# Second expert layer: output product with the activations stationary, in halves of 256 tokens

## The chip, the cores and the metric

The kernel runs on one core of a Trainium2 chip. The metric is the device time of one execution in microseconds. Before the change it took 1189.61 us, the median of three runs (1189.42 to 1192.07).

## The reference

Three stages stand one behind the other, over 8192 tokens of 192 values. The first is a windowed sum over 7 neighbouring tokens with softmax weights; then come two feed-forward layers, each 192 to 2048 to 192:

```
attn = sum over k of softmax(weight_gen)[..., k] * x[token + k - 6]     # 8 heads of 24 values
y    = leaky(attn @ w_in1) @ w_out1          # leaky(h) = max(0.01 h, h)
out  = relu(y @ w_in2) ** 2 @ w_out2
```

The weights come in double precision and the result is a float32 array of 8192 x 192.

## The kernel before

The program has a recording layer: the code does not issue instructions where it stands, but records operations with an engine, an estimated cost, a priority number and the buffers that they read and write. The planner then issues them (method `issue` of `Plan`). On TensorE the order is strictly that of the priorities; on the other engines the planner may take a later operation when the first in the list could not start yet, by its own estimates. Buffers stand in rings: tag `ph` has two PSUM buffers of two banks each, and the four accumulators `q0` to `q3` of the output product have one bank each, so all eight PSUM banks are in use.

The 8192 tokens are cut into 16 blocks `tb` of `N` = 512. A *phase* is one layer on one block; it has `NPR` = 8 *steps* `j`, and in each step 256 of the 2048 hidden values of the block are made. Phases run (layer 1, blocks 0 to 4), then layer 2 and layer 1 in turn, then layer 2 on the last five blocks: 32 phases, 256 steps. In a step,

- `mm1` multiplies the input by the hidden weights into `ph`, which has 128 partitions (hidden values) by 2 banks by 512 tokens;
- `activate` makes the activations on ScalarE: `g` exactly, `gh` rounded to the format of the products; VectorE makes the remainder `gl = g - gh`;
- `mm2`, `LAG` = 2 steps later, multiplies `gh` and `gl` by the output weights into the four accumulators.

Each factor is split into a high and a low part (suffixes h and l), and three of the four products are taken: high by high, low by high, high by low. Every product contracts over 64 partitions: matmuls come in **pairs**, one on partitions 0 to 63 and one on 64 to 127 (`HALVES`), each with its own weight load of 128 columns. `mm1` has 9 terms, thus 9 pairs in a step; `mm2` has 10 pairs, in four operations: `gh` by the high and low weights for `pa` (4 pairs), `gh` for `pb` (2), `gl` for `pa` (2), `gl` for `pb` (2). In every one of these pairs weights are stationary and 512 tokens move. A step has 19 pairs, 38 matmuls and 38 weight loads.

At the end of a layer-2 phase, `end2` copies two of the accumulators to SBUF on ScalarE, adds the other two on VectorE, moves half of one result to other partitions with a DMA, transposes both, and stores the output with six DMAs. The next phase's first `mm2` waits until the four accumulators have been read.

Of the kernel before, what the change touches and what calls it, by code (L numbers as in the profile page):

```python
# [141 lines left out]
def kernel(  # L142
# [70 lines left out]

    wi = []

    wo = []

    def weight_tiles(pool, l):
# [31 lines left out]
    def piece(kind, l, j, nj, pr, dma=False, gate=()):  # L250
        n = nj * 3 * P
        pool, rings = (sb, (("raw", 2), ("w", 4))) if l else (sg, (("raw0", 4), ("w0", 8)))
        raw = pl.buf(pool, [P, SW, 2], I32, "raw", *rings[0])
        wu = pl.buf(pool, [P, SW], F32, "wu", *rings[1])
        wa = pl.buf(pool, [P, SW], F32, "wa", *rings[1])
        first_op = len(pl.ops)
        done = Buf()
        js = slice(j, j + nj)
        for i in range(j, j + nj):
            (wi_b, wo_b)["io".index(kind)][l][i] = done  # L260

        if kind == "i":
            src = (w_in1, w_in2)[l].rearrange("(s p) (n e m) w -> p s n e (m w)", p=Q, e=2, m=P)
            for d in range(2):

                def load(d=d):
                    to = raw.t[HALVES[d], :n, :].rearrange("p (s q m) w -> p s q (m w)", s=3, m=P)
                    for q in range(nj):
                        nc.sync.dma_start(out=to[:, :, q], in_=src[:, :, j + q, d])

                pl.op("SP", 0.5 * nj, pr - 6, [], [raw], load, late=(nj * 0.6, 3.5), after=gate[:1])
        else:
            src = (w_out1, w_out2)[l].rearrange("(f p) e w -> p f e w", p=P)

            def load():
                nc.sync.dma_start(
                    out=raw.t[:, :n, :].rearrange("p (f e) w -> p f e w", e=D), in_=src[:, 2 * j : 2 * (j + nj)]
                )

            pl.op("SP", 0.5, pr - 6, [], [raw], load, late=(nj * 1.2, 3.0), after=gate[:1])  # L280

        def V(b):
            return b.t[:, :n]

        def I(b):
            return b.t[:, :n].bitcast(I32)

        pl.op(
            "ACT", act(n), pr - 3, [raw], [wu, wa],
            lambda: nc.scalar.activation(V(wu), raw.t[:, :n, 1].bitcast(F32), AF.Copy, scale=2.0**-112),  # L290
            after=gate[-1:],
        )
        pl.op(
            "DVE", dve2(n), pr - 2, [wu], [wa],
            lambda: nc.vector.tensor_scalar(  # L295
                I(wa), I(wu), 3, 0x7FFFFFF8, op0=ALU.logical_shift_left, op1=ALU.bitwise_and
            ),
        )
        pl.op(
            "DVE", dve(n), pr - 2, [wu, wa], [wa],  # L300
            lambda: nc.vector.scalar_tensor_tensor(  # L301
                I(wa), I(wu), SIGN, I(wa), op0=ALU.bitwise_and, op1=ALU.bitwise_or
            ),
        )
        pl.op(
            "DVE", dve2(n), pr - 2, [wa], [wu],
            lambda: nc.vector.tensor_scalar(I(wu), I(wa), SIGN_EXP, None, op0=ALU.bitwise_and),  # L307
        )
        pl.op(
            "DVE", dve(n), pr - 2, [wu, raw], [wu],  # L310
            lambda: nc.vector.scalar_tensor_tensor(  # L311
                V(wu), raw.t[:, :n, 0].bitcast(U32), 2.0**-52, V(wu), op0=ALU.mult, op1=ALU.mult
            ),
        )
        if dma:
            plus(wa, lambda: V(wa), wu, lambda: V(wu), pr - 2, (nj * 0.8, 4.5))
        else:
            pl.op(
                "DVE", dve(n), pr - 2, [wu, wa], [wa],
                lambda: nc.vector.tensor_tensor(V(wa), V(wa), V(wu), op=ALU.add),  # L320
            )
        def to(hl):
            if kind == "i":
                return wi[l][hl][:, :, js, :].rearrange("p s q m -> p s (q m)")
            return wo[l][:, 2 * j : 2 * (j + nj), slice(0, D) if hl == "h" else slice(D, 2 * D)]

        def val():
            return V(wa).rearrange("p (s m) -> p s m", s=3 if kind == "i" else 2 * nj)

        def high():  # L330
            if l:
                second()
            nc.scalar.copy(to("h"), val())  # L333

        hb = Buf()
        pl.op("ACT", act(n), pr - 1, [wa], [hb], high, after=tuple(borrowed) if l else ())
        parts = [(slice(None), slice(None))]
        if kind == "o":
            parts = [(slice(Q, D), slice(0, P)), (slice(0, Q), slice(P, D))]
        for ts, cs in parts:  # L340
            o = pl.op(
                "DVE", dve(n // len(parts)), pr - 1, [wa, hb], [done],
                lambda ts=ts, cs=cs: nc.vector.tensor_tensor(  # L343
                    to("l")[:, :, ts], val()[:, :, cs], to("h")[:, :, cs].bitcast(F32), op=ALU.subtract
                ),
            )
        if l == 0:
            borrowed.extend(pl.ops[first_op:])
        return o
# [4 lines left out]
    wg_flat = weight_gen.rearrange("b s h k -> (b s) (h k)").rearrange(  # L354
        "(a b i t) e -> i a b (t e)", a=A, i=BI, t=TB
    )
    out_rows = out.rearrange("(a b u) d -> a b u d", a=A, u=BI * TB)
    out_flat = out.rearrange("(a b i t) d -> i t a b d", a=A, i=BI, t=TB)
    FULL = (HALO + TB) * D

# [174 lines left out]
    g_t = {}  # L535
    acc_t = {}

    def mm1(l, tb, j, pr):
        xs = sets[l, tb]
        ph = h_t[l, tb, j] = pl.buf(ps, [P, 2, N], F32, "ph", "ph", 2)  # L540

        def go():
            wh, wl = wi[l]["h"], wi[l]["l"]

            terms = [(w, hl, s) for ss in ("ab", "s") for w, hl in ((wh, "h"), (wl, "h"), (wh, "l")) for s in ss]
            for i, (w, hl, s) in enumerate(terms):
                for d in range(2):
                    c = 2 if s == "b" else d ^ (s == "s")
                    nc.tensor.matmul(  # L549
                        ph.t[:, d, :],  # L550
                        lhsT=w[HALVES[d], c, j, :],
                        rhs=xs[s + hl].t[HALVES[d]],
                        start=(i == 0),
                        stop=(i == len(terms) - 1),
                    )

        return pl.op("PE", 9 * MM, pr, [*xs.values(), wi_b[l][j]], [ph], go)

    def activate(l, tb, j, pr):
        ph = h_t.pop((l, tb, j))  # L560
# [17 lines left out]
    def mm2(l, tb, j, pr):  # L578
# [26 lines left out]
                lambda terms=terms, g=g, n=n: prods(terms, g, first and n < 2, last and n >= 2),  # L605
            )
        if last:
            (end1, end2)[l](tb, acc, pr - 1)


    def total(acc, i, v, hold, pr):
# [7 lines left out]
    def wide(name, ring=("w", 4)):  # L619
        return pl.buf(sb, [P, N], F32, name, *ring)  # L620
# [32 lines left out]
        )  # L653
        halves(xs, "b", lambda: bu.t, bu, pr - 1)

    def end2(tb, acc, pr):
        oa, ob, bw = wide("oa", ("e", 2)), wide("ob", ("e", 2)), wide("bw")
        total(acc, 0, oa, [], pr)
        total(acc, 1, ob, [bw], pr)
        ta = pl.buf(sb, [P, N], F32, "ta", "c", 2)  # L660
        pl.op("SP", 0.5, pr, [ob], [bw], lambda: nc.sync.dma_start(out=bw.t[0:Q], in_=ob.t[Q:P]), late=(0.5, 2.0))
        pl.op("DVE", dve(N), pr + 1, [oa], [ta], lambda: nc.vector.transpose(ta.t, oa.t))

        def store(src, c0, n):
            for c in range(n):
                v = src.t[32 * c : 32 * c + 32].rearrange("a (u e) -> a u e", e=32)
                nc.sync.dma_start(out=out_rows[:, tb, :, 32 * (c0 + c) : 32 * (c0 + c + 1)], in_=v)

        pl.op("SP", 2.0, pr + 1, [ta], [], lambda: store(ta, 0, 4), late=(1.0, 2.0))
        pl.op(  # L670
            "DVE", dve(N), pr + 2, [ob, bw], [ob],
            lambda: nc.vector.tensor_tensor(ob.t[0:Q], ob.t[0:Q], bw.t[0:Q], op=ALU.add),
        )
        pl.op("DVE", dve(N), pr + 2, [ob], [oa], lambda: nc.vector.transpose(oa.t[0:Q], ob.t[0:Q]))
        pl.op("SP", 1.0, pr + 2, [oa], [], lambda: store(oa, 4, 2), late=(0.5, 2.0))


    phases = [(0, tb) for tb in range(LEAD)]
# [27 lines left out]
    with tc.manual_schedule():  # L706
# [13 lines left out]
        for i in range(len(steps) + LAG):  # L720
            if i < len(steps):
                l, tb, j = steps[i]
                q = i // NPR + 1
                if j == (LAG if i >= NPR else 0) and q < len(phases):
                    gate = starts[q - 2 : q - 1] if q > 2 else ()
                    lq, tq = phases[q]
                    if lq:
                        again(tq, at[lq, tq] - 3, gate)
                    else:
                        local_sum(tq, at[lq, tq] - (4 if tq >= EARLY else 6), gate)  # L730
                o = mm1(l, tb, j, i)
                if j == 0:
                    starts.append(o)
                activate(l, tb, j, i + 0.5)
            if i >= LAG:
                mm2(*steps[i - LAG], i + 0.5)
        pl.issue()
    Plan.last = pl

# [29 lines left out]
```

## Time and profile before

| | |
|---|---|
| median of 3 runs | 1189.61 us |
| profiled execution, its time | 1188.75 us |
| its span, first to last instruction | 1187.0 us |
| TensorE (PE) busy | 1139.3 us, 96%, 9748 matmuls |
| weight loads (PEld) busy | 919.8 us, 77%, 9748 loads |
| VectorE (DVE) busy | 725.3 us, 61% |
| ScalarE (ACT) busy | 749.3 us, 63% |
| granted TensorE clock, mean | 0.989 |

A matmul's recorded time runs from its start to the end of its pipeline, so matmuls overlap in the record: the distance between the starts of two pairs is what counts, not the duration. The same holds for weight loads. The granted clock is 1.00 (2.4 GHz) or 0.50 (1.2 GHz).

### The profile page before, as it was taken

To read this page: it belongs to the slowest core of one execution; us is meant where nothing else is said; L and a number is where in the kernel's file an instruction comes from. 1 tells how busy PE (TensorE), PEld (TensorE's weight loads), DVE (VectorE), ACT (ScalarE), POOL (GpSimd) and SP (SyncE) were. 2 spreads that over 40 slices of the span, in tenths; PEclk is the share of its full clock that TensorE was granted. 3 is DMA by queue.
4 is the path that set the end of the run, shared out by engine and by line. 5 is a ranking of instruction groups with operands and counts; after the bars stand their busy time and mean duration, and the time that the engine had idled before them with its cause. 6 is when DMAs were issued, how large, how long until landed. Compare 5 with 4: busy or idle time off the path is not lost.

```text
span 1187.0 us, 22999 instructions
## 1 busy us (share of the span) xinstructions
PE 1139.3 (96%) x9748; PEld 919.8 (77%) x9748; DVE 725.3 (61%) x871; ACT 749.3 (63%) x830; POOL 15.7 (1%) x20
## 2 busy tenths in 40 slices
PE   2699999999999999999999999999999999999997
PEld 1478787887888888788887888888788888888885
DVE  7999999848465474745648475564846543344333
ACT  2555566574756748575674857657575674777774
POOL 0210000000000000000000000000000000000000
PEclk9799999999999999999999999999999999999999
DMA  8954646051512314142131513214151231121111
GB/s 185 221 105 105 157 129 171 14 136 20 146 21 79 71 42 127 19 124 44 56 95 36 131 19 101 62 32 123 20 148 19 85 79 44 58 63 36 19 19 18
DMA packets 112798, 94.29 MB, mean 79 GB/s; under 512 B 59644, under 2 KB 89114, under 8 KB 112696
## 3 DMA queue, kind: packets, MB, share of 16 engines
q1 hardware_dynamic: 108712, 87.99, 29.6%
q0 software_dynamic: 3792, 4.72, 2.5%
q8 instruction: 76, 1.25, 0.4%
q14 instruction: 26, 0.21, 0.1%
q10 hardware_dynamic: 192, 0.11, 0.0%
HBM read 50.06 MB, written 20.19 MB: 59 GB/s over the span
## 4 chain that ended last, share of the span: by engine, by line
PE 90%; DVE 6%; issue 1%; ACT 1%; DMA 1%; SPq 0%; POOL 0%; DVEq 0%; POOLq 0%; ACTq 0%
PE ph L549 43%; PE pa L591 29%; PE pb L591 19%; DVE gl L574 1%; DVE tmp L471 1%; DVE att L483 1%; DVE wa L301 1%; DVE wu L311 0%; DVE wu L307 0%; DVE wa L295 0%; DMA xc<-in_x_dram 0%; DVE wo L343 0%; DMA wg<-in_weight_gen_dram 0%; ACT wu L290 0%; DMA bw<-ob 0%
## 5 line engine op out<-in xcount | busy, mean ns | idle before, releaser
L574 DVE TENSOR_TENSOR gl<-g,gh 128x1024 fp32r<-128x1024 f32 x256 | 312.7, 1223 | 391.0 <-ACT g L571 292.7
L566 ACT ACTIVATE gh<-ph 128x1024 fp32r<-128x1024 f32 x128 | 131.7, 1029 | 262.3 <-PE ph L549 262.3
L591 PE MATMUL pa<-gh,wo 64*128 64x512 f32 x2048 | 280.3, 392 | 2.0 <-DVE s L615 1.9
L591 PEld LDWEIGHTS pa<-gh,wo 64*128 64x128 f32 x2048 | 191.5, 185 | 50.0 <-DVE oa L615 3.5
L569 ACT ACTIVATE g<-ph 128x1024 f32<-128x1024 f32 x128 | 131.6, 1028 | 119.7 <-PE ph L549 119.7
L591 PE MATMUL pa<-gl,wo 64*128 64x512 f32 x1024 | 159.9, 390 | 0.6 <-DVE gl L574 0.6
L591 PE MATMUL pb<-gh,wo 64*128 64x512 f32 x1024 | 159.9, 390 | 0.0
L591 PE MATMUL pb<-gl,wo 64*128 64x512 f32 x1024 | 159.5, 389 | 0.0
L571 ACT ACTIVATE g<-g 128x1024 f32<-128x1024 f32 x128 | 136.1, 1063 | 3.5
L570 ACT ACTIVATE gh<-g 128x1024 fp32r<-128x1024 f32 x128 | 135.7, 1060 | 4.0
L567 ACT ACTIVATE g<-ph 128x1024 f32<-128x1024 f32 x128 | 130.7, 1021 | 0.2 <-DVE gl L574 0.2
L591 PEld LDWEIGHTS pa<-gl,wo 64*128 64x128 f32 x1024 | 96.1, 184 | 22.9 <-DVE gl L574 1.1
L591 PEld LDWEIGHTS pb<-gh,wo 64*128 64x128 f32 x1024 | 96.1, 184 | 22.3 <-DVE wo L343 0.5
L591 PEld LDWEIGHTS pb<-gl,wo 64*128 64x128 f32 x1024 | 96.2, 184 | 21.9
L471 DVE TENSOR_TENSOR tmp<-xc,wg 128x768 f32<-128x768 f32 x96 | 91.1, 949 | 0.0
L483 DVE TENSOR_TENSOR att<-att,tmp 128x768 f32<-128x768 f32 x91 | 86.9, 955 | 1.7
L549 PE MATMUL ph<-xah,wi0h 64*128 64x512 f32 x256 | 52.4, 405 | 8.9 <-ACT wi0h L333 8.9
L549 PE MATMUL ph<-xah,wi0l 64*128 64x512 f32 x256 | 52.4, 405 | 2.5 <-DVE wi0l L343 2.5
L549 PE MATMUL ph<-xbl,wi0h 64*128 64x512 f32 x256 | 51.8, 401 | 0.9 <-DVE xbl L406 0.9
L549 PE MATMUL ph<-xbh,wi0l 64*128 64x512 f32 x256 | 51.9, 402 | 0.0
L549 PE MATMUL ph<-xbh,wi0h 64*128 64x512 f32 x256 | 51.6, 400 | 0.0
L549 PE MATMUL ph<-xal,wi0h 64*128 64x512 f32 x256 | 51.6, 399 | 0.0
(98 smaller groups left out, 1450.7 us busy)
## 6 DMA issues: line engine op xcount, KB each, us to landing
xc<-in_x_dram SPq DMA_DIRECT2D x62, 240.0 KB, 4.5
xsh<-xah SPq DMA_DIRECT2D x60, 128.0 KB, 2.4
xsl<-xal SPq DMA_DIRECT2D x60, 128.0 KB, 2.4
raw<-in_moe_w_in_dram SPq DMA_DIRECT2D x32, 192.0 KB, 6.3
raw<-in_moe_w_out_dram SPq DMA_DIRECT2D x7, 768.0 KB, 4.8
sc<-xb SPq DMA_DIRECT2D x14, 384.0 KB, 2.3
ka<-s SPq DMA_DIRECT2D x16, 256.0 KB, 2.0
kb<-s SPq DMA_DIRECT2D x16, 256.0 KB, 3.1
```

What stands on the lines that cost most here:

```text
L301: lambda: nc.vector.scalar_tensor_tensor(I(wa), I(wu), SIGN, I(wa), op0=ALU.bitwise_and, op1=ALU.bitwise_or),
L471: nc.vector.tensor_tensor(dst, xk, wg.t[:, :, :, k : k + 1].to_broadcast([P, TB, H, G]), op=ALU.mult)
L483: lambda tmp=tmp: nc.vector.tensor_tensor(acc(), acc(), tmp.t, op=ALU.add),
L549: nc.tensor.matmul(ph.t[:, d, :], lhsT=w[HALVES[d], c, j, :], rhs=xs[s + hl].t[HALVES[d]], start=(i == 0), stop=(i == len(terms) - 1),)
L566: pl.op("ACT", W, pr, [ph], [gh], lambda: nc.scalar.activation(gh.t, ph.t, AF.Prelu, alpha=0.01))
L567: pl.op("ACT", W, pr, [ph], [g], lambda: nc.scalar.activation(g.t, ph.t, AF.Prelu, alpha=0.01))
L569: pl.op("ACT", W, pr, [ph], [g], lambda: nc.scalar.activation(g.t, ph.t, AF.Relu))
L570: pl.op("ACT", W, pr, [g], [gh], lambda: nc.scalar.activation(gh.t, g.t, AF.Square))
L571: pl.op("ACT", W, pr, [g], [g], lambda: nc.scalar.activation(g.t, g.t, AF.Square))
L574: lambda: nc.vector.tensor_tensor(gl.t, g.t, gh.t.bitcast(F32), op=ALU.subtract),
L591: nc.tensor.matmul(acc[d][w == "b"].t, lhsT=wt[:, {"ah": slice(0, P), "b": slice(P, 2 * P), "al": slice(2 * P, 3 * P)}[w]], rhs=g.t[HALVES ...
```

## The change

In layer 2 alone, the output product turns its factors round: 128 tokens of the activations become the stationary operand, and the output weights move, 384 columns for `gh` (192 high and 192 low) and 192 for `gl` (the high ones). The results come out with tokens on partitions, so the transposes at the end fall away. An accumulator now holds 128 tokens by 384 columns; the four of them hold 256 tokens, in the two partition halves' parts `d`. So layer 2 works on halves `u` of 256 tokens: in a step, `mm1` makes the hidden values of two former steps (512 of them) for 256 tokens, by 18 pairs of 256 columns each, and four steps complete a half. `mm2_turned` has 8 pairs of 384 columns and 8 of 192. The new `end2` runs twice in a phase.

```diff
@@ piece: no reordering of the low weights in layer 2
-        if kind == "o":
+        if kind == "o" and l == 0:
@@ mm1
+    def parts(l, j):
+        if l == 0:
+            return [(slice(0, N), j, slice(0, N))]
+        u, jj = divmod(j, NPR // 2)
+        return [(slice(HN * e, HN * e + HN), 2 * jj + e, slice(HN * u, HN * u + HN)) for e in range(2)]
...
-            for i, (w, hl, s) in enumerate(terms):
...
-                    nc.tensor.matmul(
-                        ph.t[:, d, :],
-                        lhsT=w[HALVES[d], c, j, :],
-                        rhs=xs[s + hl].t[HALVES[d]],
...
+            for to, jw, cols in parts(l, j):
+                for i, (w, hl, s) in enumerate(terms):
...
+                        nc.tensor.matmul(
+                            ph.t[:, d, to],
+                            lhsT=w[HALVES[d], c, jw, :],
+                            rhs=xs[s + hl].t[HALVES[d], cols],
...
@@ new: the output product of layer 2
+    def mm2_turned(tb, j, pr):
+        gh, gl = g_t.pop((1, tb, j))
+        u, jj = divmod(j, NPR // 2)
+        first, last = jj == 0, jj == NPR // 2 - 1
...
+        jobs = [(e, c) for e in range(2) for c in range(2)]
+        def prods(q, g, width, begin, end):
+            for i, (e, c) in enumerate(jobs):
+                for d in range(2):
+                    o = HN * e + P * q
+                    nc.tensor.matmul(
+                        acc[d][q].t[:, 0:width],
+                        lhsT=g.t[HALVES[d], c, o : o + P],
+                        rhs=wo[1][HALVES[d], 2 * (2 * jj + e) + c, 0:width],
...
+        for n, (g, width, cost) in enumerate(((gh, 2 * D, 0.176), (gl, D, 0.107))):
+            for q in range(2):
+                pl.op(
+                    "PE", 4 * cost, pr + 0.02 * n + 0.01 * q, [g, *ws], [a[q] for a in acc],
+                    lambda q=q, n=n, g=g, width=width: prods(q, g, width, first and n == 0, last and n == 1),
+                )
+        if last:
+            end2(tb, u, acc, pr - 1)
@@ end2, new: twice per phase, for 256 tokens
+    def end2(tb, u, acc, pr):
+        v = pl.buf(sb, [P, 2, 2 * D], F32, "v", "w", 4)
+        for q in range(2):
+            pl.op(
+                "ACT", act(2 * D), pr, [acc[1][q]], [v],
+                lambda q=q: nc.scalar.copy(v.t[:, q], acc[1][q].t[:, 0 : 2 * D]),
+            )
+        for q in range(2):
+            pl.op(
+                "DVE", dve(2 * D), pr, [acc[0][q], v], [v],
+                lambda q=q: nc.vector.tensor_tensor(v.t[:, q], acc[0][q].t[:, 0 : 2 * D], v.t[:, q], op=ALU.add),
+            )
+        pl.op(
+            "DVE", dve(2 * D), pr, [v], [v],
+            lambda: nc.vector.tensor_tensor(v.t[:, :, 0:D], v.t[:, :, 0:D], v.t[:, :, D:], op=ALU.add),
+        )
...
+                nc.sync.dma_start(out=out_flat[2 * u + q][:, :, tb], in_=v.t[:, q, 0:D])
```

On TensorE, in the middle of a layer-2 phase, one step stands so before: nine input pairs (`ph`, here by their two matmuls, x2), then the output product (`pa`, `pb`) of two steps earlier. Sizes are partitions by moving columns.

```order
L549 MATMUL ph<-xal,wi1h 128x512 x2
L549 MATMUL ph<-xbl,wi1h 128x512 x2
L549 MATMUL ph<-xsh,wi1h 128x512 x2
L549 MATMUL ph<-xsh,wi1l 128x512 x2
L549 MATMUL ph<-xsl,wi1h 128x512 x2
L591 MATMUL pa<-gh,wo_1025 128x512 x8
L591 MATMUL pb<-gh,wo_1025 128x512 x4
L591 MATMUL pa<-gl,wo_1025 128x512 x4
L591 MATMUL pb<-gl,wo_1025 128x512 x4
```

And so after the change, from the fifth pair of the step's second set of nine (the first set, the same nine rows, stands ahead of it):

```order
L561 MATMUL ph<-xal,wi1h 128x256 x2
L561 MATMUL ph<-xbl,wi1h 128x256 x2
L561 MATMUL ph<-xsh,wi1h 128x256 x2
L561 MATMUL ph<-xsh,wi1l 128x256 x2
L561 MATMUL ph<-xsl,wi1h 128x256 x2
L637 MATMUL po<-wo_1025,gh 128x384 x16
L637 MATMUL po<-wo_1025,gl 128x192 x16
```

The step goes from 38 matmuls with as many weight loads to 68; the order of the two products against each other stays.

On ScalarE, in the middle of a layer-2 phase of the changed kernel, the two accumulator copies of the first half (`v<-po`) stand between the second and the third activation of a step:

```order
L581 ACTIVATE g<-ph 128x1024
L582 ACTIVATE gh<-g 128x1024
L583 ACTIVATE g<-g 128x1024
L581 ACTIVATE g<-ph 128x1024
L582 ACTIVATE gh<-g 128x1024
L706 COPY v<-po 128x384 x2
L583 ACTIVATE g<-g 128x1024
```

Before, no copy stood in the middle of a phase there; the one set of copies stood behind the phase's last step, among the next phase's activations, where the second half's copies stand now too.

On VectorE the last instructions of the program were these before (`ob<-ob,bw` adds what the DMA brought, and two transposes stand around it):

```order
L574 TENSOR_TENSOR gl<-g,gh 128x1024 x6
L615 TENSOR_TENSOR oa<-pa,oa 128x512
L615 TENSOR_TENSOR ob<-pb,ob 128x512
L662 STREAM_TRANSPOSE ta<-oa 128x512
L672 TENSOR_TENSOR ob<-ob,bw 64x512
L674 STREAM_TRANSPOSE oa<-ob 64x512
```

and are these after:

```order
L586 TENSOR_TENSOR gl<-g,gh 128x1024 x4
L711 TENSOR_TENSOR v<-po,v 128x384 x2
L715 TENSOR_TENSOR v<-v 128x2x192
L586 TENSOR_TENSOR gl<-g,gh 128x1024 x3
L711 TENSOR_TENSOR v<-po,v 128x384 x2
L715 TENSOR_TENSOR v<-v 128x2x192
```

The transposes and the wait for a DMA are gone from the end, and the short sums stand there twice, once for each half of 256 tokens.

## Rows read from the trace of the kernel before

**Rows 1.** The page: span, and busy time by engine (share of the span, instructions).

```profile
span 1187.0 us, 22999 instructions
...
PE 1139.3 (96%) x9748; PEld 919.8 (77%) x9748; DVE 725.3 (61%) x871; ACT 749.3 (63%) x830; POOL 15.7 (1%) x20
```

**Rows 2.** The page: chain that ended last, by engine and by line.

```profile
PE 90%; DVE 6%; issue 1%; ACT 1%; DMA 1%; SPq 0%; POOL 0%; DVEq 0%; POOLq 0%; ACTq 0%
PE ph L549 43%; PE pa L591 29%; PE pb L591 19%; DVE gl L574 1%; DVE tmp L471 1%; DVE att L483 1%; DVE wa L301 1%; DVE wu L311 0%; DVE wu L307 0%; DVE wa L295 0%; DMA xc<-in_x_dram 0%; DVE wo L343 0%; DMA wg<-in_weight_gen_dram 0%; ACT wu L290 0%; DMA bw<-ob 0%
```

**Rows 3.** Timeline of PE, two layer-2 steps (start us, us, engine, line, form).

```profile
596.57 0.39 PE L549 MATMUL ph<-xah,wi1h 64*128 64x512 f32 x2
...
600.87 0.39 PE L549 MATMUL ph<-xah,wi1h 64*128 64x512 f32 x2
...
605.18 0.39 PE L549 MATMUL ph<-xah,wi1h 64*128 64x512 f32 x2
```

**Rows 4.** Timeline of PE, layer 1, eight pairs apart.

```profile
566.04 0.39 PE L549 MATMUL ph<-xbh,wi0h 64*128 64x512 f32 x2
...
567.91 0.40 PE L591 MATMUL pa<-gh,wo 64*128 64x512 f32 x2
```

**Rows 5.** Timeline of PE at the start of the program, four pairs apart.

```profile
36.99 0.62 PE L549 MATMUL ph<-xbh,wi0l 64*128 64x512 f32 x2
...
38.69 0.63 PE L549 MATMUL ph<-xsh,wi0l 64*128 64x512 f32 x2
```

**Rows 6.** Windows (stretch, length, busy of PE, PEld, DVE, ACT, POOL, clock, DMA share, GB/s).

```profile
36.50:39.00 2.50, 2.50 (x12) 2.01 (x14) 2.46 (x6) 0.00 (x0) 1.21 (x1) 0.50 1.09 251
...
550.00:576.00 26.00, 26.00 (x224) 20.72 (x222) 22.16 (x28) 12.95 (x15) 0.00 (x0) 1.00 0.12 21
1040.00:1170.00 130.00, 130.00 (x1150) 107.45 (x1148) 52.63 (x56) 100.73 (x104) 0.00 (x0) 1.00 0.16 32
```

**Rows 7.** Timeline of PE and PEld after a wait at full clock: one pair, two pairs.

```profile
52.24 0.19 PEld L591 LDWEIGHTS pa<-gl,wo 64*128 64x128 f32 x2 [1.08 <-DVE gl L574]
52.24 0.30 PEld L591 LDWEIGHTS pa<-gl,wo 64*128 64x128 f32 x4 [1.08 <-DVE gl L574]
52.24 0.50 PE L591 MATMUL pa<-gl,wo 64*128 64x512 f32 x2 [0.64 <-DVE gl L574]
```

**Rows 8.** Timeline, the program's first weight load and first matmul.

```profile
21.53 0.18 PEld L496 LDWEIGHTS pt<-ident,att 128*128 128x128 f32 x1 [21.53 <-issue]
...
21.56 0.45 PE L496 MATMUL pt<-ident,att 128*128 128x128 f32 x1 [21.56 <-DVE att L483]
```

**Rows 9.** Groups by line and shape, adds and copies at a layer-2 phase's end (busy, mean ns).

```profile
L615 DVE TENSOR_TENSOR oa<-pa,oa 128x512 f32<-128x512 f32 x16 | 11.0, 686 | 11.1 <-ACT oa L612 11.1
...
L612 ACT COPY oa<-pa 128x512 f32<-128x512 f32 x16 | 9.3, 583 | 3.1 <-PE pa L591 3.1
```

**Rows 10.** Waits in total (us, times, longest), weight loads for the accumulators.

```profile
PEld pa L591 <- DVE oa L615: 3.5, 11, 0.3
```

**Rows 11.** Timeline of a step's end in layer 2: input product, activation.

```profile
1166.63 0.39 PE L549 MATMUL ph<-xsl,wi1h 64*128 64x512 f32 x2
...
1167.06 1.03 ACT L569 ACTIVATE g<-ph 128x1024 f32<-128x1024 f32 x1 [1.09 <-PE ph L549]
```

**Rows 12.** Timeline: weights for the next windowed sum, their load and first use.

```profile
601.28 1.98 SPq L423 DMA_DIRECT2D wg<-in_weight_gen_dram  x4
...
619.62 0.38 DVE L447 TENSOR_REDUCE mx<-wg 128x32 f32<-128x224 f32 x1
```

**Rows 13.** Timeline of the last microseconds, all engines.

```profile
1177.51 0.61 PE L591 MATMUL pb<-gl,wo 64*128 64x512 f32 x4
...
1179.54 0.70 DVE L662 STREAM_TRANSPOSE ta<-oa 128x512 f32<-128x512 f32 x1
...
1181.99 0.68 DVE L672 TENSOR_TENSOR ob<-ob,bw 64x512 f32<-64x512 f32 x1 [1.75 <-DMA bw<-ob]
...
1183.44 0.85 SPq L667 DMA_DIRECT2D out_dram<-oa  x2
```

More of the change, by code (lines that the diff above doesn't have):

```diff
@@ L356 @@
     )
-    out_rows = out.rearrange("(a b u) d -> a b u d", a=A, u=BI * TB)
     out_flat = out.rearrange("(a b i t) d -> i t a b d", a=A, i=BI, t=TB)
@@ L536 @@
     acc_t = {}
+    HN = N // 2
+    def parts(l, j):
[3 more added lines that the diff above has]
+        return [(slice(HN * e, HN * e + HN), 2 * jj + e, slice(HN * u, HN * u + HN)) for e in range(2)]
     def mm1(l, tb, j, pr):
@@ L545, in go @@
             terms = [(w, hl, s) for ss in ("ab", "s") for w, hl in ((wh, "h"), (wl, "h"), (wh, "l")) for s in ss]
-            for i, (w, hl, s) in enumerate(terms):
-                for d in range(2):
-                    c = 2 if s == "b" else d ^ (s == "s")
-                    nc.tensor.matmul(
-                        ph.t[:, d, :],
-                        lhsT=w[HALVES[d], c, j, :],
-                        rhs=xs[s + hl].t[HALVES[d]],
[L553 to L557, printed above, removed]
+            for to, jw, cols in parts(l, j):
+                for i, (w, hl, s) in enumerate(terms):
+                    for d in range(2):
+                        c = 2 if s == "b" else d ^ (s == "s")
+                        nc.tensor.matmul(
+                            ph.t[:, d, to],
+                            lhsT=w[HALVES[d], c, jw, :],
+                            rhs=xs[s + hl].t[HALVES[d], cols],
+                            start=(i == 0),
+                            stop=(i == len(terms) - 1),
+                        )
+        return pl.op("PE", 9 * MM, pr, [*xs.values(), *(wi_b[l][jw] for _, jw, _ in parts(l, j))], [ph], go)
     def activate(l, tb, j, pr):
@@ L607, in mm2 @@
         if last:
-            (end1, end2)[l](tb, acc, pr - 1)
+            end1(tb, acc, pr - 1)
+    def mm2_turned(tb, j, pr):
+        gh, gl = g_t.pop((1, tb, j))
+        u, jj = divmod(j, NPR // 2)
+        first, last = jj == 0, jj == NPR // 2 - 1
+        if first:
+            acc_t[1] = [[pl.buf(ps, [P, N], F32, "po", f"q{2 * d + q}", 1) for q in range(2)] for d in range(2)]
+        acc = acc_t[1]
+        jobs = [(e, c) for e in range(2) for c in range(2)]
+        def prods(q, g, width, begin, end):
+            for i, (e, c) in enumerate(jobs):
+                for d in range(2):
+                    o = HN * e + P * q
[3 more added lines that the diff above has]
+                        rhs=wo[1][HALVES[d], 2 * (2 * jj + e) + c, 0:width],
+                        start=begin and i == 0,
+                        stop=end and i == len(jobs) - 1,
+                    )
+        ws = [wo_b[1][2 * jj + e] for e in range(2)]
+        for n, (g, width, cost) in enumerate(((gh, 2 * D, 0.176), (gl, D, 0.107))):
[6 more added lines that the diff above has]
+            end2(tb, u, acc, pr - 1)
     def total(acc, i, v, hold, pr):
@@ L654, in again, with store @@
         halves(xs, "b", lambda: bu.t, bu, pr - 1)
[L656 to L669, printed above, removed]
+    def end2(tb, u, acc, pr):
[9 more added lines that the diff above has]
+                lambda q=q: nc.vector.tensor_tensor(v.t[:, q], acc[0][q].t[:, 0 : 2 * D], v.t[:, q], op=ALU.add),
+            )
         pl.op(
-            "DVE", dve(N), pr + 2, [ob, bw], [ob],
-            lambda: nc.vector.tensor_tensor(ob.t[0:Q], ob.t[0:Q], bw.t[0:Q], op=ALU.add),
-        )
-        pl.op("DVE", dve(N), pr + 2, [ob], [oa], lambda: nc.vector.transpose(oa.t[0:Q], ob.t[0:Q]))
-        pl.op("SP", 1.0, pr + 2, [oa], [], lambda: store(oa, 4, 2), late=(0.5, 2.0))
+            "DVE", dve(2 * D), pr, [v], [v],
+            lambda: nc.vector.tensor_tensor(v.t[:, :, 0:D], v.t[:, :, 0:D], v.t[:, :, D:], op=ALU.add),
+        )
+        def store():
+            for q in range(2):
+                nc.sync.dma_start(out=out_flat[2 * u + q][:, :, tb], in_=v.t[:, q, 0:D])
+        pl.op("SP", 1.0, pr + 1, [v], [], store, late=(0.5, 2.0))
     phases = [(0, tb) for tb in range(LEAD)]
@@ L735 @@
             if i >= LAG:
-                mm2(*steps[i - LAG], i + 0.5)
+                l, tb, j = steps[i - LAG]
+                if l:
+                    mm2_turned(tb, j, i + 0.5)
+                else:
+                    mm2(l, tb, j, i + 0.5)
         pl.issue()
```

## The prediction, made before the changed kernel ran

> **What bounds the kernel now.** I read the page first: TensorE is busy 96% of the span, and 90% of the chain that ended last lies on it, all of that on the two product lines [rows 1, 2]. VectorE and ScalarE stand near 60% over the span. In the stretch that is layer 2 alone, ScalarE works 100.73 of 130 us (77%) and VectorE 52.63 (40%), with TensorE busy throughout and the clock at 1.00 [rows 6]. So a layer-2 step is worth what its pairs of matmuls cost, as long as the others keep up.
>
> The timeline gives that cost. Two layer-2 steps take 605.18 - 596.57 = 8.61 us [rows 3]; a step is 4.305 us, and with 19 pairs a pair takes **226.6 ns**. In layer 1 eight pairs take 1.87 us, 234 ns each, with the same shapes at the same full clock [rows 4, 6]. At the half clock (1.2 GHz) four pairs take 1.70 us, 425 ns each [rows 5, 6]; 512 columns at 1.2 GHz are 426.7 ns, so there the stream of columns is all that counts. At 2.4 GHz the stream would be 213.3 ns. So at full clock each pair carries a **surcharge** over its stream: 13.3 ns in layer 2 and about 20.5 ns in layer 1.
>
> Is it a price per column or per weight load? Layers 1 and 2 differ in these pairs in where the weights lie and in the numbers themselves; counts, widths and the moving tiles' rings are alike. A difference of 7 ns that follows the weights points to the load. I therefore take the surcharge as one per pair, whatever its width. This is the main choice in the sum.
>
> A second floor shows where the array resumes after a wait at full clock. The first pair is recorded 0.50 us long instead of the usual 0.39, so its columns began 0.11 us after its load; and two pairs' loads end 0.30 us after the first's start while one takes 0.19, so the second load began 0.11 us after the first [rows 7]. A pair thus can't come sooner than about **110 ns** after the one ahead of it, the time in which its weights get ready.
>
> **The sum, part by part.**
>
> *Input product.* 9 pairs of 512 columns become 18 of 256, with twice the loads. 256 columns stream in 106.7 ns; with 13.3 a pair takes 120 ns, just over the load's floor. 18 x 120 = 2.160 us, against 9 x 226.6 = 2.039: **+0.121 us** a step.
>
> *Output product.* 10 pairs of 512 become 8 of 384 (160 + 13.3 = 173.3 ns) and 8 of 192 (80 + 13.3 = 93.3, so the floor of 110 holds). 1.387 + 0.880 = 2.267 us against 2.266: **nothing**. The columns fall from 5120 to 4608, and the six more loads eat it.
>
> So a step goes from 4.305 to 4.426 us; over 128 layer-2 steps that is **+15.5 us**.
>
> *Stationary activations.* The output product's loads now read `gh` and `gl`, which no load of before does. The two values known are 13.3 and 20.5 ns; the floor covers them for the narrow pairs (80 + 20.5 is under 110). On 8 wide pairs the upper value is 7.2 x 8 x 128 = 7.4 us; I take the middle, **+3.7 us**.
>
> Here the Trainium skill speaks for the change: its page "TensorE: Matmul & The Clock Gate", section Back-to-back issue gap, prices an isolated matmul at full clock at its columns over 2.4 GHz plus 2.5 ns, that is 109, 162.5 and (by the load) 110 ns for the three widths. By it a step would be 4.14 us, and the sum some 24 us under before. The trace does not agree at 512 columns: the page's 215.8 ns are 226.6 in rows 3.
>
> *ScalarE and VectorE.* A half's four accumulators need two copies and two adds of 384 columns, and one add of 2 x 192. ScalarE's order puts the copies behind the second activation of a step. With T for the start of the input product's last pair, the first activation starts at T + 0.43 and takes 1.03 [rows 11]; two such end near T + 2.5; the output product that closes the half ends about then. Two copies (under 0.58 each, the price at 512 columns) and two adds (under 0.69) [rows 9] overlap each other, so the first bank is free near T + 3.8 and the second near T + 4.4. The next half's first output product starts one input product later, near T + 0.1 + 2.27 + 2.16 = T + 4.5, and reaches its second bank 0.7 us after that. No wait, therefore, but slack of some 0.7 us; if the copies slipped behind the third activation (1.03 us), about 0.4 us would be lost at 16 places, 6 us. At the phase's end the accumulators' old wait, 3.5 us in 11 waits [rows 10], stays at most. ScalarE gains some 0.7 us per phase, which its 23% of free time covers. These cost nothing in the sum.
>
> *Transfers.* Six stores and a copy by DMA per phase become four stores; the DMA engines are 16% busy there [rows 6]. SyncE issues in order, and the first half's stores now stand ahead of the loads for the next windowed sum. They wait for a half that ends some 29 us into the phase, against 22 us, where the first of those loads (`wg`) was issued before; `wg` was first read 18 us after that [rows 12]. The slack covers the 7 us.
>
> *The end.* Now 9.0 us lie between the last pair's start (1177.51 + about 0.45) and the end of the span at 1187.0: an add, a transpose, a DMA round trip that VectorE waits 1.75 us for, an add, a transpose, a store [rows 13]. After: copy (0.55), add (0.6), short sum (0.55), two stores issued, and the same 2.7 us from the last issue's end (1184.3) to the end of the span. With 0.8 for the issues and the first matmul tail this is about 6 us: **-3 us**.
>
> Sum against the profiled execution's own 1188.75 us: +15.5 + 3.7 - 3 = +16.2, **1205 us**. The profiled execution lies 0.9 us under the median of the runs, which I let stand.
>
> **The rivals.**
>
> *The surcharge goes with the columns, or fades (faster).* If 13.3 ns on 512 columns is 2.6 ns per hundred, pairs take 113.3, 170 and 110 ns: a step of 4.28 us, -3.2 - 3 = 1182.5 us. If it vanished for all three widths, with the floor of 110 left: 1.98 + 1.28 + 0.88 = 4.14 us, 1165 us. It decides for faster where the surcharge on the 26 wider pairs is under 9.5 ns: 18 x (106.7 + s) + 8 x (160 + s) + 880 = 4305 + 23 (the end's 3 us per step). For it: no row shows a narrow pair at full clock. Against it: layer 1 against layer 2.
>
> *The dear loads (slower still).* With layer 1's 20.5 ns on all wider pairs a step is 18 x 127.2 + 8 x 180.5 + 880 = 4.61 us: +39.5 - 3, 1225 us. Instructions could bind at the same height: the program's first matmul follows its load by 0.03 us [rows 8]; four instructions to a pair are 0.12 us, 68 x 2 x 0.03 = 4.1 us a step, hidden just now; at 0.034 us each they would be the bound.
>
> *A load must end before the next pair (far slower).* Recorded loads last 0.19 us [rows 7]. Were that, with 3 ns to the next start, the least distance, 34 pairs at 0.19 make 6.5 us a step: +2.15 x 128, about 1460 us. Against it stands the second load of rows 7, which began before the first had ended.
>
> The same page and section of the Trainium skill names a rule on this side: in a sustained stream of loads and matmuls it gives 81 ns per matmul at 128 columns and 131 at 512, so that narrow ones hardly get cheaper. By it, scaled to the 113 ns per matmul of this trace, a step would rise by about 1.55 us, to 1387 us. No run here shows such a floor yet.
>
> *No change.* A surcharge near 9.5 ns, or the end gaining more: 1186 to 1193 us.
>
> **How the numbers follow.** Chances: the forecast (surcharge 13 to 18 ns per pair, 1195 to 1214 us) 0.48; dear loads or instructions (1214 to 1245) 0.14; load must end 0.03; no change 0.08; per column or fading (1160 to 1186) 0.27. A measurement of this kernel tells 0.3%, 3.6 us, from no change. So faster 0.27, same 0.08, slower 0.65. The likeliest case has its own range of 1195 to 1214; the range for 8 in 10 takes in most of the faster case and of the dearer one, 1170 to 1240.
>
> **What would show it.** In the changed trace's timeline: the distance of pairs in a layer-2 step, 0.120 us for 256 columns, 0.173 for 384, 0.110 for 192; a step of 4.43 us; no new wait of TensorE on the copies (L706) or adds (L711); layer 1's 234 ns as before; about 6 us from the last matmul to the end. The forecast is wrong if 256-column pairs stand at 0.113 us or less, or if the loads or the sequencer hold the narrow pairs above 0.13 us.

## The result, and the profile after

The changed kernel takes **1202.64 us** (median of 4 runs, 1202.22 to 1205.76), the kernel before 1190.84 on the same chip (1189.42 to 1193.33). The ratio is 1.011, with a 95% interval of 1.0094 to 1.0127: slower by 1.1%, and inside the range of the forecast. The execution that was profiled is the longest of the four, 1205.76 us; where its last 3 us come from is read below.

The page of the changed kernel: its span, the busy time of the engines, and the chain that ended last, by engine and by line (of before: [rows 1, 2]).

```profile
span 1204.0 us, 30628 instructions
...
PE 1157.0 (96%) x13588; PEld 1079.5 (90%) x13588; DVE 725.6 (60%) x883; ACT 757.1 (63%) x862; POOL 15.7 (1%) x20
...
PE 91%; DVE 6%; issue 1%; ACT 1%; DMA 0%; SPq 0%; POOL 0%; DVEq 0%; POOLq 0%; ACTq 0%
PE ph L561 44%; PE po L637 24%; PE pa L603 14%; PE pb L603 9%; DVE gl L586 1%; DVE tmp L471 1%; DVE att L483 1%; DVE wa L302 1%; DVE wu L312 0%; DVE wu L308 0%; DVE wa L296 0%; DMA xc<-in_x_dram 0%; DVE wo L344 0%; ACT wu L291 0%; DVE wi0l L344 0%
```

TensorE bounds it as before, and by as much of its span. It runs 3840 matmuls more, and its weight loads take 90% of the span instead of 77%. So the question is again what a pair costs. TensorE's timeline over one step of layer 2 shows it (start, us, line, form; it answers to [rows 3]):

```profile
1180.77 1.57 PE L637 MATMUL po<-wo,gh 64*128 64x384 f32 x16
1182.16 1.05 PE L637 MATMUL po<-wo,gl 64*128 64x192 f32 x16
1183.03 0.33 PE L561 MATMUL ph<-xah,wi1h 64*128 64x256 f32 x2
1183.17 0.30 PE L561 MATMUL ph<-xbh,wi1h 64*128 64x256 f32 x2
...
1185.09 0.30 PE L561 MATMUL ph<-xsl,wi1h 64*128 64x256 f32 x2
1185.20 0.36 PE L637 MATMUL po<-wo,gh 64*128 64x384 f32 x2
```

Eight wide pairs take 1182.16 - 1180.77 = 1.39 us, 174 ns each. Eight narrow ones take 0.87 us, 109 ns each. The 18 input pairs take 2.17 us: 120 ns each, but the first, behind the narrow ones, 0.14 us. The step is 4.43 us, where it was 4.305. The output product alone is as long as before (2.26 against 2.27 us); the input product is longer by 0.13. Layer 1's steps take 4.45 us, as before.

Two windows of the changed kernel, the stretch of [rows 6] in layer 2, and one early in the program (stretch, length, busy of PE, PEld, DVE, ACT, POOL, clock, DMA share, GB/s):

```profile
80.00:90.00 10.00, 8.00 (x50) 6.07 (x52) 8.91 (x12) 4.08 (x7) 0.00 (x0) 0.83 0.00 0
...
1040.00:1170.00 130.00, 130.00 (x1998) 130.00 (x1996) 51.11 (x59) 99.70 (x109) 0.00 (x0) 1.00 0.12 34
```

and the early window of the kernel before:

```profile
80.00:90.00 10.00, 9.16 (x74) 7.28 (x76) 9.90 (x13) 4.89 (x7) 0.00 (x0) 1.00 0.01 2
```

In layer 2 TensorE waits for nothing at full clock, and VectorE, ScalarE and the DMA engines do a little less than before. The early window, where the program is the same, differs by itself: TensorE is busy for 1.16 us less, and its mean clock is 0.83. One input product of layer 1 and the output product behind it show what that costs, in the changed kernel and in the kernel before:

```profile
83.31 0.73 PE L561 MATMUL ph<-xah,wi0h 64*128 64x512 f32 x2
87.06 1.09 PE L603 MATMUL pa<-gh,wo 64*128 64x512 f32 x8
```

```profile
81.51 0.50 PE L549 MATMUL ph<-xah,wi0h 64*128 64x512 f32 x2
83.72 1.10 PE L591 MATMUL pa<-gh,wo 64*128 64x512 f32 x8
```

The product begins 1.80 us later, behind longer waits, and takes 3.75 us instead of 2.21. These 3.3 us are the whole difference at the first step of layer 2, which begins at 230.90 us, in the profile before at 227.61. They are no part of what layer 2 does; in the traces of runs 1, 2 and 3 below, whose layer 1 is unchanged too, that step begins at 233.34, 229.45 and 227.99 us.

ScalarE and VectorE at the point where a half closes in mid-phase, in the changed kernel (in brackets the idle time ahead, and what ended it):

```profile
1182.05 1.06 ACT L582 ACTIVATE gh<-g 128x1024 fp32r<-128x1024 f32 x1
1183.01 0.84 ACT L706 COPY v<-po 128x384 f32<-128x384 f32 x2
1183.74 1.07 ACT L583 ACTIVATE g<-g 128x1024 f32<-128x1024 f32 x1
1183.51 1.02 DVE L711 TENSOR_TENSOR v<-po,v 128x384 f32<-128x384 f32 x2 [2.49 <-ACT v L706]
1184.56 0.56 DVE L715 TENSOR_TENSOR v<-v 128x384 f32<-128x384 f32 x1
```

The copies stand behind the second activation, as ordered, and both accumulators are read by 1183.51 + 1.02 = 1184.53. The next half's first output pair starts at 1185.20. So TensorE has at least 0.67 us to spare; the first pair's operation needs only the first two accumulators, and the add that reads the last of them ends at 1184.06, 1.14 us ahead. No wait of TensorE on L706 or L711 is on the list of waits.

The last microseconds of the changed kernel (of before: [rows 13]):

```profile
1196.27 0.40 PE L637 MATMUL po<-wo,gl 64*128 64x192 f32 x4
1196.27 0.93 ACT L706 COPY v<-po 128x384 f32<-128x384 f32 x2 [3.19 <-PE po L637]
1196.78 1.02 DVE L711 TENSOR_TENSOR v<-po,v 128x384 f32<-128x384 f32 x2 [2.44 <-ACT v L706]
1197.84 0.56 DVE L715 TENSOR_TENSOR v<-v 128x384 f32<-128x384 f32 x1
1198.42 1.12 SPq L720 DMA_DIRECT2D out_dram<-v  x2
```

From the last matmul's end (1196.67) to the end of the span are 7.3 us; by the same reading it was 8.9. The copies and adds are as short as reckoned. The two issues took 1.12 us instead of 0.8, and 4.4 us pass from the end of the last issue (1199.54) to the end of the span, where 2.7 did.

The account of the profiled executions: from the first layer-2 step's start to the last matmul's end 965.8 us against 950.5, +15.3; the end -1.6; the start +3.3. Together that is the 17.0 us between the spans.

### The profile page after: what moved, and what is told of

It is laid out like the page before. It is cut to its first block, busy times and chain, and to the rows that moved or that the text cites. A ratio compares the mean times of both kernels' runs of the same rounds, so it can differ in the third digit from the quotient of the medians.

```text
span 1204.0 us, 30628 instructions
## 1 busy us (share of the span) xinstructions
PE 1157.0 (96%) x13588; PEld 1079.5 (90%) x13588; DVE 725.6 (60%) x883; ACT 757.1 (63%) x862; POOL 15.7 (1%) x20
## 4 chain that ended last, share of the span: by engine, by line
PE 91%; DVE 6%; issue 1%; ACT 1%; DMA 0%; SPq 0%; POOL 0%; DVEq 0%; POOLq 0%; ACTq 0%
PE ph L561 44%; PE po L637 24%; PE pa L603 14%; PE pb L603 9%; DVE gl L586 1%; DVE tmp L471 1%; DVE att L483 1%; DVE wa L302 1%; DVE wu L312 0%; DVE wu L308 0%; DVE wa L296 0%; DMA xc<-in_x_dram 0%; DVE wo L344 0%; ACT wu L291 0%; DVE wi0l L344 0%
## 5 line engine op out<-in xcount | busy, mean ns | idle before, releaser
L637 PE MATMUL po<-wo,gh 64*128 64x384 f32 x2048 | 202.4, 333 | 0.0
L637 PEld LDWEIGHTS po<-wo,gh 64*128 64x128 f32 x2048 | 178.6, 185 | 0.9
L603 PE MATMUL pa<-gh,wo 64*128 64x512 f32 x1024 | 145.3, 397 | 1.9 <-DVE s L660 1.8
L637 PE MATMUL po<-wo,gl 64*128 64x192 f32 x2048 | 134.7, 268 | 0.0
L637 PEld LDWEIGHTS po<-wo,gl 64*128 64x128 f32 x2048 | 134.7, 187 | 0.0
L603 PEld LDWEIGHTS pa<-gh,wo 64*128 64x128 f32 x1024 | 103.3, 186 | 18.6 <-DVE s L660 2.7
L561 PE MATMUL ph<-xah,wi1h 64*128 64x256 f32 x512 | 80.3, 288 | 0.0
L561 PE MATMUL ph<-xbl,wi1h 64*128 64x256 f32 x512 | 78.2, 280 | 0.0
L561 PE MATMUL ph<-xsl,wi1h 64*128 64x256 f32 x512 | 78.2, 280 | 0.0
L561 PE MATMUL ph<-xbh,wi1l 64*128 64x256 f32 x512 | 78.2, 280 | 0.0
```

The lines of the kernel that those rows point to most:

```text
L561: nc.tensor.matmul(ph.t[:, d, to], lhsT=w[HALVES[d], c, jw, :], rhs=xs[s + hl].t[HALVES[d], cols], start=(i == 0), stop=(i == len(terms) - 1),
L603: nc.tensor.matmul(acc[d][w == "b"].t, lhsT=wt[:, {"ah": slice(0, P), "b": slice(P, 2 * P), "al": slice(2 * P, 3 * P)}[w]], rhs=g.t[HALVES ...
L637: nc.tensor.matmul(acc[d][q].t[:, 0:width], lhsT=g.t[HALVES[d], c, o : o + P], rhs=wo[1][HALVES[d], 2 * (2 * jj + e) + c, 0:width], start= ...
```

## The experiments

Theory: the loss is the halving of the input product, at about 13 ns for each pair, however wide. Rivals: the new output product costs time and something else gives it back; the surcharge goes with something other than pairs; the layers' 234 and 226.6 ns have a cause that changes what the loss rests on.

**1. The input product in halves, and nothing else** (from the kernel before).

```diff
+            spans = [slice(0, N // 2), slice(N // 2, N)] if l else [slice(0, N)]
+            for cols in spans:
...
-                        ph.t[:, d, :],
+                            ph.t[:, d, cols],
...
-                        rhs=xs[s + hl].t[HALVES[d]],
+                            rhs=xs[s + hl].t[HALVES[d], cols],
```

> The kernel before with one part of the change: layer 2's input product alone goes in 18 pairs of 256 columns instead of 9 of 512 (each pair of before cut in two, with its weights loaded twice); the output product, its end and the order of the work stay as before. Theory (a surcharge of 13.3 ns per pair, whatever its width): pairs at 120 ns instead of 226.6, +0.12 us in each of 128 layer-2 steps, +15 us, about 1206 us. Rival (the surcharge goes with the columns): 113 ns, 0 us. Rival (the output product is what made the changed kernel slower): 0 us here.

Measured: 1210.24 us, ratio 1.0165 (1.015 to 1.0181). TensorE's timeline of this kernel, one layer-2 step:

```profile
600.98 1.09 PE L593 MATMUL pa<-gh,wo 64*128 64x512 f32 x8
...
603.27 0.28 PE L551 MATMUL ph<-xah,wi1h 64*128 64x256 f32 x2
603.38 0.28 PE L551 MATMUL ph<-xbh,wi1h 64*128 64x256 f32 x2
...
605.42 0.40 PE L593 MATMUL pa<-gh,wo 64*128 64x512 f32 x2
```

18 pairs take 605.42 - 603.27 = 2.15 us, 0.11 over the nine of before, and the output product ahead of them 603.27 - 600.98 = 2.29 us, 0.02 more than before. A phase of eight steps is 1.00 us longer (35.64 against 34.65): 16 us over the 16 phases, a little more than the changed kernel's 15.3. The other 4 us or so (5.7 in the profiled executions) lie ahead of layer 2, whose first step begins at 233.34 us. There TensorE stood idle for longer and then ran at the half clock (window of this kernel):

```profile
80.00:90.00 10.00, 6.80 (x30) 4.82 (x32) 9.75 (x14) 4.08 (x7) 0.00 (x0) 0.66 0.00 0
```

SyncE's issues of the first weights for the windowed sum took 3.76 us there, against 1.81 before and 2.65 in the changed kernel; what lengthened them stays open, since that part of the program is not changed.

**2. Narrow pairs cut in half** (from the changed kernel; half of the products with `gl` is left out).

```diff
-        for n, (g, width, cost) in enumerate(((gh, 2 * D, 0.176), (gl, D, 0.107))):
+        for n, (g, width, cost) in enumerate(((gh, 2 * D, 0.176), (gl, D // 2, 0.107))):
```

> The changed kernel with half of the work of the narrow pairs left out: the low activations multiply 96 of the 192 weight columns (half of that correction is missing from the output). Theory (a pair can't come sooner than 110 ns after the last, the time in which its weights get ready): pairs stay at about 109 ns, no change, 1203 us. Rival (192 columns' stream plus a surcharge of 28 ns): 40 ns less on 8 pairs in 128 steps, 41 us faster, about 1162 us.

Measured: 1203.51 us, ratio to before 1.0108 (1.0094 to 1.0123), the time of the changed kernel. Its timeline:

```profile
1178.86 1.58 PE L637 MATMUL po<-wo,gh 64*128 64x384 f32 x16
1180.25 1.01 PE L637 MATMUL po<-wo,gl 64*128 64x96 f32 x16
...
1181.26 0.31 PE L561 MATMUL ph<-xbh,wi1h 64*128 64x256 f32 x2
...
1183.30 0.51 PE L637 MATMUL po<-wo,gh 64*128 64x384 f32 x3
```

The step is 1183.30 - 1178.86 = 4.44 us with half of the narrow columns gone, and from the second on narrow pairs still stand 108 to 112 ns apart. The second starts 46 ns behind the first, and the first input pair behind them takes as much longer: from the first narrow pair to the second input pair it is 1.01 us here (1181.26 - 1180.25) and in the changed kernel (1183.17 - 1182.16). The floor that [rows 7] showed holds: below some 110 ns a pair gets no cheaper.

**3. The turned output product over whole blocks and all 128 rows** (from the kernel before): the input product stays at 512 columns, and single matmuls take the place of pairs.

```diff
+                nc.tensor.matmul(
+                    acc[q].t[:, 0:width],
+                    lhsT=g.t[:, c, P * q : P * q + P],
+                    rhs=wo[1][:, 2 * j + c, 0:width],
...
+                if l:
+                    mm2_turned(tb, j, i + 0.5)
```

> The other part of the change alone: layer 2's output product is turned round, but contracts over 128 partitions in one matmul instead of two pairs of 64, so that four accumulator banks hold a whole block of 512 tokens and the input product keeps its 9 pairs of 512 columns. Per step 8 matmuls of 384 and 8 of 192 columns with 16 loads, where the changed kernel has twice as many over 64 partitions. Theory (one load and its stream count once, however many partitions): output product 2.27 us as before and in the changed kernel, the end some 2 us shorter: 1186 to 1190 us. Rival (changing between products over 64 and over 128 partitions empties the array, twice a step): 0.2 us or more each, 50 us slower or worse. Rival (one matmul instead of two saves the surcharge): 8 x 11 ns x 128 = 11 us faster, 1177 us.

Measured: 1240.76 us, ratio 1.0421 (1.0407 to 1.0436). Its timeline, an output product and the input product behind it:

```profile
611.56 1.68 PE L665 MATMUL po<-wo,gh 128*128 128x384 f32 x8
613.07 1.03 PE L665 MATMUL po<-wo,gl 128*128 128x192 f32 x8
614.03 0.50 PE L549 MATMUL ph<-xah,wi1h 64*128 64x512 f32 x2
614.37 0.39 PE L549 MATMUL ph<-xbh,wi1h 64*128 64x512 f32 x2
614.60 0.40 PE L549 MATMUL ph<-xah,wi1l 64*128 64x512 f32 x2
...
615.98 0.39 PE L549 MATMUL ph<-xsl,wi1h 64*128 64x512 f32 x2
616.30 0.44 PE L665 MATMUL po<-wo,gh 128*128 128x384 f32 x1
```

Single matmuls over 128 rows stand as far apart as the pairs (177 and 112 ns), so the output product is no dearer by its width. But each change between 64 and 128 rows is paid on both of its sides. The first input pair takes 0.34 us and the last 0.32, where one takes 0.227; the eight wide matmuls take 1.51 us, where 8 x 177 ns are 1.42, and the eight narrow ones 0.96, where 8 x 112 are 0.90. The input product grows from 2.04 to 2.27 us and the output product by as much: some 0.4 us a step, so about 0.2 us for each of its two changes, and about 50 us in all. The Trainium skill says that a change of tiling mode drains the array ("TensorEngine Tiling (Array Packing)", section Tiling Modes) and gives no price; the delay of 0.2 us at each change agrees with it.

**4. Layer 1's weights shifted by 32 bytes** (from the kernel before). The forecast rests on a reading of the two layers' 234 and 226.6 ns; the next runs ask what that difference is.

```diff
+    const.tile([P, 8], F32, name="gap0")
     weight_tiles(const, 0)
+    const.tile([P, 8], F32, name="gap1")
```

> The kernel before with nothing changed but the place of layer 1's three weight tiles in SBUF, 32 bytes further on (two unused tiles of 32 bytes around them, so that all else moves by 64). Layer 1's weights lay at multiples of 64 bytes, layer 2's, the inputs and the activations lie 32 bytes off such multiples. Theory (the surcharge comes from the weight load, and the 7 ns between the layers from where the weights lie): layer 1's pairs fall from 234 to 227 ns, 19 x 128 x 7.3 ns = 18 us off, about 1172 us. Rival (the numbers in the tiles, or what else runs beside layer 1): no change, 1190 us.

Measured: 1188.04 us, ratio 0.998 (0.9969 to 0.9991). A layer-1 step still takes 565.74 - 561.31 = 4.43 us, where it was 4.45. The shift took off some 2 us, not the 18 of this theory, which fell:

```profile
561.31 0.39 PE L551 MATMUL ph<-xah,wi0h 64*128 64x512 f32 x2
...
565.74 0.40 PE L551 MATMUL ph<-xah,wi0h 64*128 64x512 f32 x2
```

**5. Layer 1's input product in halves** (from the kernel before; the edit of run 1, for layer 1 alone).

```diff
+            spans = [slice(0, N // 2), slice(N // 2, N)] if l == 0 else [slice(0, N)]
```

> The kernel before with layer 1's input product, not layer 2's, cut into 18 pairs of 256 columns. Layer 1's pairs of 512 columns carry 20.5 ns over their stream. Theory (all of a surcharge is per pair): pairs at 127 ns, +0.18 us in 128 steps, 23 us slower, about 1213 us. Rival (13.3 per pair as in layer 2, the further 7 ns with the columns): 123.6 ns, +0.12 us, 16 us slower, 1206 us. Rival (the further 7 ns come only at 512 columns): 120 ns, +0.05 us, 7 us slower, 1197 us.

Measured: 1193.55 us, ratio 1.0026 (1.0011 to 1.004). Its timeline, an input product of layer 1:

```profile
561.47 0.28 PE L551 MATMUL ph<-xah,wi0h 64*128 64x256 f32 x2
561.59 0.28 PE L551 MATMUL ph<-xbh,wi0h 64*128 64x256 f32 x2
...
563.58 1.10 PE L593 MATMUL pa<-gh,wo 64*128 64x512 f32 x8
```

18 pairs take 2.11 us here, and 2.13 in the mean of layer 1's steps, where nine took 2.11 before. Halving costs layer 1 next to nothing, because its pairs of 256 columns lose the extra 7 ns that its pairs of 512 carry: they stand 115 to 121 ns apart, not 127. With 118 ns in the mean they carry 11 ns over their stream of 106.7, even less than layer 2's.

**6. Layer 1's weights placed behind the other tiles** (from the kernel before). Inputs and activations move down by the weights' 48 KB in each partition.

```diff
-    weight_tiles(const, 0)
     wi_b = [[None] * NPR for _ in range(2)]
...
+    weight_tiles(ctx.enter_context(tc.tile_pool(name="const0", bufs=1)), 0)
     stage = ExitStack()
```

> The kernel before with layer 1's three weight tiles in another part of SBUF: from byte 130848 of each partition on, above the inputs and activations and below layer 2's weights, instead of from 17536 on, below them; the inputs and activations move down by 49152 bytes, nothing else changes. The move by 32 bytes left layer 1's pairs at 233 ns. Theory (the 7 ns between the layers come from the part of SBUF in which the weights lie): layer 1's pairs fall to about 227 ns, up to 18 us off, 1172 us. Rival (not the place, but the numbers or the layer's other work): layer 1 stays at 233 to 234 ns, 1190 us.

Measured: **1174.36 us**, ratio 0.9865 (0.9842 to 0.9889). Its timeline, a layer-1 step:

```profile
540.89 0.39 PE L549 MATMUL ph<-xah,wi0h 64*128 64x512 f32 x2
...
542.93 1.07 PE L591 MATMUL pa<-gh,wo 64*128 64x512 f32 x8
...
545.20 0.39 PE L549 MATMUL ph<-xah,wi0h 64*128 64x512 f32 x2
```

The step takes 4.31 us, layer 2's own price: nine pairs in 2.04, ten in 2.27. Layer 1's extra cost was one of placement, and this kernel beats both.

**7. Only layer 1's output weights placed there** (from the kernel before). It asks whether the cost goes with the stationary tile itself.

```diff
-    weight_tiles(const, 0)
+    wi.append({k: const.tile([P, 3, NPR, P], F32R, name=f"wi0{k}") for k in "hl"})
...
+    wo.append(ctx.enter_context(tc.tile_pool(name="const0", bufs=1)).tile([P, NFC, 2 * D], F32R, name="wo0"))
```

> The kernel before with only layer 1's output weights moved up (from byte 155424 on); its input weights stay at 17536, below the inputs and activations, which move down by 24576 bytes. Theory (each pair's surcharge follows the place of its own stationary tile): layer 1's output pairs fall to 227 ns, its input pairs stay near 233; about 10 x 128 x 7 ns = 9 us off, 1181 us. Rival (it is the place of the moving tiles, which also moved): both products change alike, all of 16 us or nothing.

Measured: 1184.46 us, ratio 0.9951 (0.9937 to 0.9966), two thirds of the gain expected. Its timeline, a layer-1 step that begins with the output product, and ahead of it an output product of layer 1 that stands in layer 2's first step of a phase:

```profile
298.19 1.07 PE L592 MATMUL pa<-gh,wo 64*128 64x512 f32 x8
...
300.45 0.39 PE L550 MATMUL ph<-xah,wi1h 64*128 64x512 f32 x2
...
542.25 1.09 PE L592 MATMUL pa<-gh,wo 64*128 64x512 f32 x8
...
544.55 0.39 PE L550 MATMUL ph<-xah,wi0h 64*128 64x512 f32 x2
...
546.65 1.09 PE L592 MATMUL pa<-gh,wo 64*128 64x512 f32 x8
```

The output product takes 2.30 us (2.34 before, 2.27 in run 6), the input product 2.10 (2.11 before, 2.04 in run 6). So most of each product's extra goes with its own weights; but the output product kept about half of its own (its pairs stand 224 to 236 ns apart). Behind layer 2's input product the same weights cost nothing extra: 300.45 - 298.19 = 2.26 us. So what stands ahead of a product has a part in its price. The activations moved too in both runs, so that their place has a part in it is not excluded.

**8. The changed kernel with layer 1's weights placed there** (the edit of run 6).

> The changed kernel with layer 1's weight tiles moved to byte 130848 and above, as in the run before this one that took 16 us off the kernel before. Theory (layer 1's place and layer 2's narrower pairs are separate terms, one per layer): 16 us off here too, 1203 - 16 = 1187 us, still some 13 us behind the kernel before with the same move; layer 1's pairs near 227 ns, layer 2's still 120, 174 and 110. Rival (the turned product needs its own place; moving the activations down changes their loads): layer 2's 174 ns go up by as much as layer 1 gains.

Measured: 1190.71 us, ratio to before 0.9994 (0.9984 to 1.0004): 12 us under the changed kernel, less than expected. Its timeline, one step of layer 1:

```profile
556.33 0.42 PE L561 MATMUL ph<-xah,wi0h 64*128 64x512 f32 x2
558.37 1.10 PE L603 MATMUL pa<-gh,wo 64*128 64x512 f32 x8
...
560.64 0.42 PE L561 MATMUL ph<-xah,wi0h 64*128 64x512 f32 x2
```

The step takes 4.31 us, as in run 6. By phases of eight steps, layer 1's fell by 0.84 us and layer 2's by 0.06, where in run 6 they fell by 0.95 and 0.20 against the kernel before; 16 x 0.25 = 4 us is the gain that is missing. It is missing where the layers meet: in the first two steps of a phase, in which one layer's input product stands with the other's output product, a step fell by 0.03 to 0.04 us, in run 6 by 0.07 to 0.10. The placement helps the changed kernel as well, but it stays 16 us behind run 6: a cheaper layer 1 makes the change no cheaper.

## Why the prediction was right

**The mechanism held.** Pairs of 256, 384 and 512 columns take 120, 174 and 226.6 ns: 13.3 ns over their stream at 2.4 GHz (106.7, 160, 213.3) at each width. In layer 2 that is a price per pair, and the surcharge that goes with columns or fades fell with it. Run 1 isolates the consequence: nine more pairs a step cost 16 us over layer 2, with the old output product in place. The forecast's term was 15.5 us, and the stretch from layer 2's first step to the last matmul, layer 1's phases between them included, grew by 15.3. That they are so close is in part luck: a step well inside layer 2 went from 4.307 to 4.440 us, which is 17.0 over 128 steps, and the first three steps of a phase grew by only 0.07 to 0.11 each.

**The output product cost nothing**, as reckoned: 8 x 174 and 8 x 109 ns are 2.26 us, against 2.27. A tenth of its columns is gone, and the six pairs more and the floor under the narrow ones eat it; run 2 shows the floor itself.

**The stationary activations** were the term that was mis-sized: 3.7 us, the middle of 0 and 7.4. The wide pairs measure 174 ns, the lower end, so it was nothing. With it falls the rival of dear loads (180.5 ns wide, 127 ns at 256 columns). The rival by which a load must end first fell too: it needed 6.5 us a step, and a step takes 4.43. The Trainium skill's figures do not fit on either side ("TensorE: Matmul & The Clock Gate", section Back-to-back issue gap): its isolated price is 109 and 162.5 ns where 120 and 174 were measured, and its sustained 81 ns at 128 columns and 131 at 512 would put a matmul of 384 between them, where run 3's single ones take 177.

**The end** gave 1.6 us instead of 3. The steps on VectorE and ScalarE took what was reckoned; the two issues took 1.12 us for 0.8, and from their end it was 4.4 us to the end of the span, not the 2.7 behind the last two stores before.

**ScalarE, VectorE and the transfers** cost nothing: where a slack of 0.7 us was reckoned, the first accumulators were read 1.14 us ahead. One thing was not foreseen: the first input pair behind the narrow pairs takes 137 to 145 ns, 0.02 us a step.

Put together, 15.3 - 1.6 on the profiled 1188.75 us is 1202.5, and the measured median is 1202.64. The three runs without a profile are 2.8 to 3.5 us shorter than the profiled one, so they may lack the early 3.3 us; no trace shows it. The forecast lay 2.4 us higher: 3.7 too much for the stationary term and 0.2 for the pairs, less the 1.4 that the end did not give. The two medians differ by only 11.8, as that of before lies 2 us over its profiled execution: the match to 0.1 us is luck, and some 2 us either way are not accounted for.

**One argument was weaker than it read.** The prediction took the surcharge as one per load because layer 1's 7 ns more "follows the weights". They do follow the weights' place: run 6 removes them, run 4 does not. But run 5 shows that they come at 512 columns and not at 256, so they are not a fixed price per load, and they say nothing about whether the other 13.3 ns are; at 256 columns layer 1's pairs carry 11. The choice was right, on evidence that did not carry it; a pair of 256 columns at full clock, which no row of before had, would have.

**What stays open.** Why weights in their old place cost 7 ns more per pair of 512 columns; why the steps where the layers meet gain less of it in run 8 than in run 6; and what lengthened SyncE's early issues in run 1.

## What to carry to other kernels

Where TensorE is the bound, count pairs as well as columns: here, in layer 2, each pair costs 13 ns above its stream, and a row of narrow ones goes no faster than about 110 ns each, so that narrower matmuls lose what fewer columns save. When two parts of a program run the same shapes at different prices, ask what differs before using the difference as evidence; here it was mostly the place of the weights, and moving them was worth 1.35%, more than the change cost. Read the same stretch of unchanged program in both traces: 3 us of the profiled difference came from there.

## What was not expected of the hardware

- The place of the stationary weights in SBUF sets the price of a pair of 512 columns: 234 ns where layer 1's lay, 226.7 behind the other tiles, with nothing else changed but where inputs and activations lie. A shift by 32 bytes takes only 0.02 us off a step of layer 1 (4.45 to 4.43), the move 0.14.
- A change between matmuls over 64 rows and over 128 rows costs about 0.2 us each way, half of it in the product that ends and half in the one that begins (run 3).
- In the step of the changed kernel that is shown the two matmuls of a pair start 23 to 24 ns apart, over most of its length 17 to 43, in the kernel before 3; the distance of pairs is the same.
- Early waits of TensorE (0.83 us to 80.06 and 1.94 us to 82.66 in the changed kernel, one of 1.21 before) were followed by a stretch at the half clock that the profile before does not have. In run 6 a wait of 1.88 us, to 82.23, was not followed by one: the clock there stayed at 1.00.
